# First matrix product of four 512-token tiles by Strassen's seven block products, weight sums streamed from memory

## The chip, the cores and the metric

The kernel runs on one core of one Trainium2 chip. The metric is device time in microseconds (us), the median of three runs. The engines are called PE (TensorE), DVE (VectorE), ACT (ScalarE), POOL (GpSimd) and SP (SyncE, which issues the DMAs).

## What is computed

The reference first computes decay attention with 4 batches, 8 heads, 768 positions and head size 64, in blocks with a carried state, then a feed-forward layer on all 3072 tokens:

```python
def _moe_ref(x, w_in, w_out):          # x 3072 x 512, w_in 512 x 2048, w_out 2048 x 512
    h = np.maximum(x @ w_in, 0.0)
    return (h * h @ w_out).astype(np.float32)
```

The change concerns the product `x @ w_in` alone.

## The kernel before

A **chunk** is 128 tokens of one batch; there are 24. The constant `SIZES` groups them into eight tiles, of 2, 3, 3, 3, 3, 3, 3 and 4 chunks. Tiles are numbered from 0. For each tile, attention fills `xh` and `xl`, a high and a low part of x whose sum is x to float32 accuracy; the weights stay in SBUF in the same two parts (`wih`, `wil`, `woh`, `wol`), each in 16 blocks of 128 hidden units. For each hidden block f, `ffn` issues:

- **first product**, `mm1` (L566): three part products (xh wih, xl wih, xh wil) of four contraction blocks each, 12 matmuls. The weight block stands still in the array and the tile's tokens stream through it: 384 columns in a tile of three chunks, 512 in one of four. The sum lies in one PSUM bank.
- **relu and square**: ACT relu out of the bank (L582), ACT square into the high part (L587), DVE square (L588), DVE low part (L589).
- **second product**, `mm2` (L572, L573, L575): for each chunk three matmuls of 512 columns into that chunk's output bank. From tile 2 on the second products of two f are issued together.

An attention chunk of the later tiles is a **turn** (`turn_over`): the scores and state updates of one chunk (L401, L408) and the values of the chunk before it (L417, L424), 128 matmuls on 64x64 pieces of the array, with DVE and ACT work behind them (L508 to L535) and a weighted copy of the next chunk's values on DVE (L439) whose data SP loads (`pn`, L442). Finished output rows are copied out of PSUM (L633) and stored (L634).

The order on each engine is made ahead of the run by a small list scheduler, `Plan.order`, from keys and estimated durations; each engine then runs its own list strictly in order. PSUM has eight banks for all of this, `in` has four load buffers.

```python
for wt, xt in ((wih[f], xh), (wih[f], xl), (wil[f], xh)):
    for cc in range(NCC):
        nc.tensor.matmul(at(h)[:, 0:n], wt[:, cc, :], xt[:, cc, 0:n], start=k == 0, stop=k == 3 * NCC - 1)
```

Of the kernel before, what the change touches and what calls it, by code (L numbers as in the profile page):

```python
# [745 lines left out]
```

## Time and profile before

| what | value |
|---|---|
| median of 3 runs | 603.98 us (603.98 to 604.13) |
| profiled execution | 603.77 us, its span 602.1 us |
| PE busy | 595.3 us (99%) |
| PE weight loads busy | 528.2 us (88%) |
| DVE busy | 312.3 us (52%) |
| ACT busy | 221.6 us (37%) |
| DMA | 49.08 MB, mean 82 GB/s |

The span runs from the first to the last instruction of the profiled execution; the 1.67 us between it and that execution's time lie outside. A matmul's recorded duration is longer than its share of the engine, since matmuls overlap: what one costs is the distance from its start to the next one's.

### The profile page before, as it was taken

How to read it: one execution, taken by the hardware profiler on the slowest of the kernel's cores; microseconds unless marked ns; L12 is line 12 of the kernel's file. 1: busy time of each engine (PE TensorE's matmuls, PEld its weight loads, DVE VectorE, ACT ScalarE, POOL GpSimd, SP SyncE). 2: the span in 40 equal slices, each digit the busy share in tenths (PEclk: the TensorE clock that was granted, in tenths of full speed). 3: DMA queues.
4: the chain of work that ended last, by engine and by line, in shares of the span. 5: the costliest groups of instructions: out<-in, count | busy, mean ns of one | idle time of the engine just before them, and what ended most of it. 6: DMA issues, size and time to landing. Idle time of an engine off the chain costs nothing.

```text
span 602.1 us, 12963 instructions
## 1 busy us (share of the span) xinstructions
PE 595.3 (99%) x5646; PEld 528.2 (88%) x5646; DVE 312.3 (52%) x665; ACT 221.6 (37%) x470; POOL 4.2 (1%) x12
## 2 busy tenths in 40 slices
PE   8999999999999999999999999999999999999997
PEld 6899889889899898998998998988988988888885
DVE  6999999756534435524454343443555432322132
ACT  5877877534223232322322323322322322222221
POOL 2000000000000000000000000000000000000000
PEclk9999999999999999999999999999999999999999
DMA  8845655443210202201122021210231000100001
GB/s 293 307 139 175 204 182 186 165 159 124 89 39 33 71 36 89 72 0 72 52 72 71 1 72 53 72 71 1 71 124 36 3 0 1 53 1 1 0 1 70
DMA packets 15897, 49.08 MB, mean 82 GB/s; under 512 B 1888, under 2 KB 2144, under 8 KB 15840
## 3 DMA queue, kind: packets, MB, share of 16 engines
q1 hardware_dynamic: 15840, 48.25, 23.2%
q8 instruction: 44, 0.72, 0.5%
q14 instruction: 13, 0.11, 0.1%
HBM read 41.95 MB, written 6.29 MB: 80 GB/s over the span
## 4 chain that ended last, share of the span: by engine, by line
PE 91%; DVE 4%; DMA 2%; ACT 2%; issue 1%; ACTq 0%; DVEq 0%; SPq 0%
PE bank L566 42%; PE bank L572 14%; PE bank L575 14%; PE bank L573 14%; PE bank L401 2%; PE bank L417 2%; PE bank L424 2%; PE bank L408 1%; DMA in<-pn 1%; PE bank L264 1%; DVE m L329 1%; DMA in<-w 1%; DVE m L331 1%; ACT half L437 1%; DVE gls L589 1%
## 5 line engine op out<-in xcount | busy, mean ns | idle before, releaser
L572 PE MATMUL bank<-woh,ghs 128*128 128x512 f32 x352 | 139.3, 396 | 0.7 <-ACT ghs L585 0.7
L573 PE MATMUL bank<-wol,ghs 128*128 128x512 f32 x352 | 137.5, 391 | 0.0
L588 DVE TENSOR_TENSOR g<-g 128x384 f32<-128x384 f32 x80 | 44.7, 558 | 151.8 <-ACT ghs L587 151.8
L566 PE MATMUL bank<-xh,wih 128*128 128x384 f32 (+2 forms) x512 | 111.1, 339 | 0.0
L582 ACT ACTIVATE g<-bank 128x384 f32<-128x384 f32 (+1 forms) x112 | 53.3, 476 | 155.3 <-PE bank L566 155.3
L566 PE MATMUL bank<-xh,wil 128*128 128x384 f32 (+2 forms) x512 | 109.6, 336 | 0.0
L566 PE MATMUL bank<-xl,wih 128*128 128x384 f32 (+2 forms) x512 | 109.5, 336 | 0.0
L566 PEld LDWEIGHTS bank<-xh,wih 128*128 128x128 f32 x512 | 89.2, 188 | 6.3
L575 PE MATMUL bank<-woh,gls 128*128 128x512 f32 x352 | 92.8, 390 | 0.0
L566 PEld LDWEIGHTS bank<-xh,wil 128*128 128x128 f32 x512 | 88.6, 188 | 2.7
L566 PEld LDWEIGHTS bank<-xl,wih 128*128 128x128 f32 x512 | 88.5, 188 | 2.7
L572 PEld LDWEIGHTS bank<-woh,ghs 128*128 128x128 f32 x352 | 66.1, 188 | 14.4 <-ACT ghs L585 1.3
L575 PEld LDWEIGHTS bank<-woh,gls 128*128 128x128 f32 x352 | 65.9, 188 | 13.9
L573 PEld LDWEIGHTS bank<-wol,ghs 128*128 128x128 f32 x352 | 66.1, 188 | 12.1
L589 DVE TENSOR_TENSOR gls<-g,ghs 128x384 fp32r<-128x384 f32 (+1 forms) x112 | 60.2, 538 | 18.2 <-ACT ghs L585 9.8
L587 ACT ACTIVATE ghs<-g 128x384 fp32r<-128x384 f32 x80 | 42.0, 525 | 43.8 <-PE bank L573 42.1
L588 DVE TENSOR_TENSOR half<-half 128x512 f32<-128x512 f32 x16 | 11.1, 692 | 55.4 <-ACT ghs L587 28.1
L582 ACT ACTIVATE half<-bank 128x512 f32<-128x512 f32 x16 | 9.6, 601 | 58.3 <-PE bank L566 55.3
L530 ACT COPY half<-bank 128x256 f32<-128x256 f32 x40 | 12.9, 376 | 46.1 <-PE bank L424 46.1
L324 ACT ACTIVATE m<-in 128x512 f32<-128x512 f32 x32 | 21.7, 678 | 10.5 <-DMA in<-w 5.3
L531 DVE TENSOR_TENSOR half<-bank,half 128x256 f32<-128x256 f32 x40 | 15.1, 419 | 13.3 <-ACT half L530 13.2
L329 DVE SCALAR_TENSOR_TENSOR m<-in,m 128x512 uint32<-128x512 uint32 x32 | 21.7, 685 | 0.1
(75 smaller groups left out, 468.3 us busy)
## 6 DMA issues: line engine op xcount, KB each, us to landing
in<-pn SPq DMA_DIRECT2D x44, 512.0 KB, 4.5
in<-w SPq DMA_DIRECT2D x32, 512.0 KB, 3.8
out<-obs SPq DMA_DIRECT2D x22, 256.0 KB, 2.1
half<-pn SPq DMA_DIRECT2D x8, 256.0 KB, 5.0
out<-m SPq DMA_DIRECT2D x1, 256.0 KB, 2.0
out<-m SPq DMA_DIRECT2D x2, 128.0 KB, 1.7
g<-lamx SPq DMA_DIRECT2D x1, 8.0 KB, 1.6
```

What stands on the lines that cost most here:

```text
L324: o = add("ACT", 0.58, lambda: nc.scalar.activation(at(m), words(1).bitcast(F32), AF.Abs), [o], [st, m])
L329: o = add("DVE", 0.6, lambda: nc.vector.scalar_tensor_tensor(out=bits(), in0=words(1), scalar=0xC0000000, in1=bits(), op0=ALU.bitwise_and, ...
L530: oc = [add("ACT", 0.27, 1, lambda r=r: nc.scalar.copy(x4(xr)[:, 2 * r:2 * r + 2], at(ys[r])[:, 0:2 * C].rearrange("p (v i) -> p v i", v=2 ...
L531: oa = [add("DVE", 0.36, 1, lambda v=v: nc.vector.tensor_tensor(out=by_v(x4(xr), v), in0=y_(ys, v), in1=by_v(x4(xr), v), op=ALU.add), oc, ...
L566: nc.tensor.matmul(at(h)[:, 0:n], wt[:, cc, :], xt[:, cc, 0:n], start=k == 0, stop=k == 3 * NCC - 1)
L572: nc.tensor.matmul(at(os_[j]), gh_()[:, sl], woh[f], start=f == 0, stop=False)
L573: nc.tensor.matmul(at(os_[j]), gh_()[:, sl], wol[f], start=False, stop=False)
L575: nc.tensor.matmul(at(os_[j]), gl_()[:, sl], woh[f], start=False, stop=f == NF - 1)
L582: orr = plan.op("ACT", ta, key - ahead, lambda: nc.scalar.activation(g_(), at(h)[:, 0:n], AF.Relu), [o1], [h, turn_, g])
L587: ogh = plan.op("ACT", ta, key, lambda: nc.scalar.activation(gh_(), g_(), AF.Square), [orr], [g] + gs[:1], before)
L588: og = plan.op("DVE", tv, key, lambda: nc.vector.tensor_tensor(out=g_(), in0=g_(), in1=g_(), op=ALU.mult), [orr, ogh], [g])
L589: ogl = plan.op("DVE", tv, key - ahead, lambda: nc.vector.tensor_tensor(out=gl_(), in0=g_(), in1=gh_(), op=ALU.subtract), [og, ogh], [g] + ...
```

## The change

The 24 chunks are regrouped into seven tiles, of 2, 3, 3, 4, 4, 4 and 4 chunks. Tiles 0 to 2 are worked as before. In tiles 3 to 6 the first product goes by Strassen's algorithm in its Winograd form, on 2x2 blocks: 256 tokens x 256 contraction elements x 128 hidden units. Two hidden blocks make a **pair** p, of which there are eight. In place of eight block products there are seven, each of six matmuls of 256 columns (three part products, two contraction blocks):

- `sums`, during tile 2, eight times: POOL rebuilds w_in of two hidden blocks from its parts (two adds), DVE forms four differences, ACT and DVE split them into two parts, and SP stores the plain blocks and the sums in a DRAM tile `wd`, 14 blocks of 256 columns (1.835 MB) for each pair.
- `combine`, once for a tile: attention leaves x unsplit (`raw`); DVE forms four sums and ACT and DVE split seven operands (L681, L684).
- `seven`, for each tile and pair: SP streams `wd[p]` into one of three buffers laid over the old w_in; PE computes the seven products in four groups g1 to g4 (12, 12, 6 and 12 matmuls, L719) into two banks X and Y. Between them ACT copies X (`o_t`) and DVE adds (`o_u`, `o_v`, `o_c22`, `c12`), since g3 and g4 add onto quarters that must have been read before. Then relu, square and split, and the second product in pieces of 12, 6 and 6 matmuls (L767).

The x buffers, the product's parts and the streams are laid over buffers of the first tiles.

```diff
-SIZES = (2, 3, 3, 3, 3, 3, 3, 4)
+SIZES = (2, 3, 3, 4, 4, 4, 4)
...
+PLAIN = 3
+Q = 2 * C
...
+    "vds": 2, "xr": 1, "raw": 1, "tst": 2, "st": 3, "gp": 2, "ms": 2, "big": 1, "sum": 1, "u": 1}
...
+COMBOS = ("A12", "S4", "A22", "A11", "S2", "S1", "S3")
...
+BLOCKS = {"B11": (0, 2), "B21": (1, 3), "B22": (4, 5), "T1": (6, 10), "T4": (7, 11), "T3": (8, 12), "T2": (9, 13)}
+WP = 14 * Q
...
+    wd = [dram.tile([P, WP], U32, name=f"wd{p}") for p in range(NF // 2)]
...
+        late = raw is not None or not alone
+        t, tv, vd, s1, xr = Buf("in"), Buf("in"), Buf("vds" if late else "half"), [Buf("s1") for _ in range(R)], raw or Buf("xr" if late else "half")
...
+            if raw is not None:
+                return [xo]
...
+    def sums(p, key):
...
+        oa = [plan.op("POOL", 1.1, key, lambda f=f, m=m: nc.gpsimd.tensor_tensor(out=at(m), in0=whole(f)[0], in1=whole(f)[1], op=ALU.add),
+                      list(ws[f][0]), [m]) for f, m in ((f0, ma), (f1, mb))]
...
+        o1 = minus(b11, b12, b11, oa, [ma, mb])
+        o3 = minus(b12, b22, b12, [o1], [mb])
+        o2 = minus(b22, b22, b11, [o3], [ma, mb])
+        o4 = minus(b21, b21, b22, [o2], [ma, mb])
+        oh = [plan.op("ACT", 0.53, key, lambda k=k, m=m: nc.scalar.copy(at(ts)[:, 2 * k * Q:2 * (k + 1) * Q], at(m)), [o], [m, ts]) for k, m, o in ((0, ma, o4), (1, mb, o2))]
+        ol = [plan.op("DVE", 0.6, key, lambda k=k, m=m: nc.vector.tensor_tensor(
+            out=at(ts)[:, (4 + 2 * k) * Q:(6 + 2 * k) * Q], in0=at(m), in1=at(ts)[:, 2 * k * Q:2 * (k + 1) * Q], op=ALU.subtract), [oh[k]], [m, ts]) for k, m in ((0, ma), (1, mb))]
+        os_ = [plan.op("SP", 1.45, key, lambda: nc.sync.dma_start(out=wd[p][:, 0:4 * Q], in_=words(win[:, f0 * 2 * DM:(f0 + 1) * 2 * DM])), list(ws[f1][0]), after=[steps[0, min(NF - 1, 2 * p + 4)]]),
+               plan.op("SP", 0.8, key, lambda: nc.sync.dma_start(
+                   out=wd[p][:, 4 * Q:6 * Q].rearrange("p (k i) -> p k i", k=2),
+                   in_=words(win[:, f1 * 2 * DM:(f1 + 1) * 2 * DM]).rearrange("p (k i) -> p k i", k=2)[:, :, Q:2 * Q]), list(ws[f1][0]), after=[steps[0, min(NF - 1, 2 * p + 4)]]),
+               plan.op("SP", 2.9, key, lambda: nc.sync.dma_start(out=wd[p][:, 6 * Q:], in_=words(at(ts))), oh + ol, [ts])]
...
+    def combine(ti, ready, raw, xc, before, key):
...
+        o1 = tt(s1_, A["A21"], A["A22"], ALU.add, ready, [raw, tmp])
+        o3 = tt(A["A21"], A["A11"], A["A21"], ALU.subtract, [o1], [raw])
+        d["A11"] = split("A11", A["A11"], ready, [raw])
+        o2 = tt(A["A11"], s1_, A["A11"], ALU.subtract, [o1, o3] + d["A11"], [raw, tmp])
+        d["S2"] = split("S2", A["A11"], [o2], [raw])
+        d["S1"] = split("S1", s1_, [o1], [tmp])
+        d["S3"] = split("S3", A["A21"], [o3], [raw])
+        d["A12"] = split("A12", A["A12"], ready, [raw])
+        o4 = tt(A["A12"], A["A12"], A["A11"], ALU.subtract, [o2] + d["A12"], [raw])
+        d["S4"] = split("S4", A["A12"], [o4], [raw])
+        d["A22"] = split("A22", A["A22"], ready, [raw])
...
+    def seven(ti, p, xc, d, os_, key, behind, carry):
+
+        st, X, Y, u, big, gp = Buf("st"), Buf("bank"), Buf("bank"), Buf("u"), Buf("big"), Buf("gp")
+        o_st = plan.op("SP", 5.2, key - 2.5 * 2 * FAST, lambda: nc.sync.dma_start(out=words(at(st)), in_=wd[p]), stored[p], [st], behind + [last_mm.get("stream")])
+        last_mm["stream"] = o_st
...
+                for a, b in ((0, 0), (0, 1), (1, 0)):
+                    for cc in range(2):
+                        nc.tensor.matmul(at(to)[:, i * Q:(i + 1) * Q], wt[a][:, cc, :], xt[b][:, cc, :], start=first and k == 0, stop=stop and k == 5, skip_group_check=True)
...
+        g1 = group([(X, 0, "A11", "B11", True, True), (X, 1, "S2", "T2", False, True)], key, [], [last_mm.get("seven")])
+        o_t = act(0.27, 0, lambda: nc.scalar.copy(quarter(u, 0), quarter(X, 0)), [g1], [X, u])
+        o_u = dve(0.33, 0, lambda: nc.vector.tensor_tensor(out=quarter(u, 1), in0=quarter(u, 0), in1=quarter(X, 1), op=ALU.add), [o_t], [X, u])
+        g2 = group([(Y, 0, "S1", "T1", True, True), (Y, 1, "S3", "T3", False, True)], key + 0.1, [], [g1])
+        o_v = dve(0.33, 0.1, lambda: nc.vector.tensor_tensor(out=quarter(u, 2), in0=quarter(u, 1), in1=quarter(Y, 0), op=ALU.add), [o_u, g2], [Y, u])
+        o_c22 = dve(0.33, 0.1, lambda: nc.vector.tensor_tensor(out=quarter(big, 3), in0=quarter(u, 2), in1=quarter(Y, 1), op=ALU.add), [o_v], [Y, u, big])
+        g3 = group([(X, 0, "A12", "B21", False, True)], key + 0.6, [o_t, o_u], [g2])
+        g4 = group([(Y, 0, "S4", "B22", False, True), (Y, 1, "A22", "T4", False, True)], key + 0.7, [o_v, o_c22], [g3])
+        last_mm["seven"] = g4
+        steps[ti, p] = g1, g4
...
+        r22 = act(0.27, 0.6, lambda: nc.scalar.activation(quarter(big, 3), quarter(big, 3), AF.Relu), [o_c22], [big])
+        r11 = act(0.27, 0.6, lambda: nc.scalar.activation(quarter(big, 2), quarter(X, 0), AF.Relu), [g3], [X, big])
+        c12 = dve(0.6, 0.7, lambda: nc.vector.tensor_tensor(
+            out=quarter(big, 0, 2).rearrange("p (n i) -> p n i", n=2), in0=quarter(u, 1).unsqueeze(1).broadcast_to([P, 2, Q]),
+            in1=quarter(Y, 0, 2).rearrange("p (n i) -> p n i", n=2), op=ALU.add), [g4], [Y, u, big])
+        sq = act(0.53, 0.8, lambda: nc.scalar.activation(quarter(big, 2, 2), quarter(big, 2, 2), AF.Square), [r11, r22], [big])
+        h1 = act(0.53, 0.8, lambda: nc.scalar.copy(quarter(gp, 2, 2), quarter(big, 2, 2)), [sq], [big, gp])
+        l1 = dve(0.6, 0.8, lambda: nc.vector.tensor_tensor(out=quarter(gp, 6, 2), in0=quarter(big, 2, 2), in1=quarter(gp, 2, 2), op=ALU.subtract), [h1], [big, gp])
+        s0 = dve(0.6, 0.8, lambda: nc.vector.scalar_tensor_tensor(out=quarter(big, 0, 2), in0=quarter(big, 0, 2), scalar=0.0, in1=quarter(big, 0, 2), op0=ALU.max, op1=ALU.mult), [c12], [big])
+        h0 = act(0.53, 0.9, lambda: nc.scalar.copy(quarter(gp, 0, 2), quarter(big, 0, 2)), [s0], [big, gp])
+        l0 = dve(0.6, 0.9, lambda: nc.vector.tensor_tensor(out=quarter(gp, 4, 2), in0=quarter(big, 0, 2), in1=quarter(gp, 0, 2), op=ALU.subtract), [h0], [big, gp])
...
+        ab = [[(j, k) for j in range(4) for k in range(2) if (place(j, k)[0] >= 2) == x] for x in (True, False)]
+        if p < NF // 2 - 1 or ti < len(TILES) - 1:
+            for x, (what, deps, dk) in enumerate(((ab[0], [h1, l1], 0.2), (ab[1][:2], [h0, l0], 0.8), (ab[1][2:], [h0, l0], 0.9))):
+                last_mm["second"] = o = plan.op(
+                    "PE", 0.685 * len(what), key + 2 * FAST + dk, lambda what=what, x=x: second(what, p == 0 and x == 0), deps, [gp] + os_, [last_mm.get("second")])
...
+            u = unit(b, c, xs[ti], j * C, key, 0.0 if ti - 1 - (j == 0) >= PLAIN else 4.0, steps[0, BEHIND] if ti == 2 else None, raw=raws[ti])
...
+                early = [o for p in range(NF // 2) for o in sums(p, begin[2] + 15 + p * 6.0)]
+            d = combine(ti, ready, raws[ti], xc, [], begin[ti] - 8.0)
...
+                seven(ti, p, xc, d, os_, begin[ti] + 2 * p * FAST, behind, None)
...
+    for ti in range(PLAIN, len(TILES) - 1):
+        for p in range(0, NF // 2, 2):
+            o, k = turns[k], k + 1
+            o.after.append(steps[ti, p][1])
+            steps[ti, p + 1][0].after.append(o)
```

The order changes in three places that the prediction speaks of. On PE, a step of the four-chunk tile 7 before stands thus (12 matmuls of the first product, then 12 of the second, of which the first three and the first L575 are shown):

```order
L566 MATMUL bank_65<-xh_101,wih_111 128x512 x4
L566 MATMUL bank_65<-xl_102,wih_111 128x512 x4
L566 MATMUL bank_65<-xh_101,wil_127 128x512 x4
L572 MATMUL bank_64<-woh_142,ghs 128x512 [waits Activation_49]
L573 MATMUL bank_64<-wol_158,ghs 128x512
L575 MATMUL bank_64<-woh_142,gls 128x512 [waits DVE_49]
```

and now, a pair of tile 3 that follows a turn (bank_75 is X, bank_74 is Y):

```order
L719 MATMUL bank_75<-xall,win 128x256 [waits DMAHW4_49,DVE_49]
L719 MATMUL bank_75<-xall,win 128x256 x11
L719 MATMUL bank_74<-xall,win 128x256 [waits DVE_49,Activation_49]
L719 MATMUL bank_74<-xall,win 128x256 x11
L719 MATMUL bank_75<-xall,win 128x256 [waits DVE_49]
L719 MATMUL bank_75<-xall,win 128x256 x5
L767 MATMUL bank_78<-woh_110,win 128x512
L767 MATMUL bank_78<-wol_126,win 128x512
L719 MATMUL bank_74<-xall,win 128x256 [waits DVE_49]
L719 MATMUL bank_74<-xall,win 128x256 x11
```

The groups g1, g2 and g3 stand directly behind one another, and g3 waits for DVE's read of X; six matmuls of the pair before stand between g3 and g4 (two are shown). In the other pairs twelve such matmuls stand between g2 and g3.

On ACT, the steps of the last three-chunk tiles before are relu and square in turn:

```order
L582 ACTIVATE g_71<-bank_68 128x384 [waits PE_49]
L534 CAST xh_99<-half_94 128x4x128 [waits DVE_49,Activation_49]
L587 ACTIVATE ghs<-g_71 128x384 [waits Activation_49]
L582 ACTIVATE g_73<-bank_64 128x384 [waits PE_49]
L587 ACTIVATE ghs<-g_73 128x384 [waits Activation_49]
```

and now, at the end of tile 3, from the copy of X of pair 7 on (L684 splits an operand of the next tile; L750 and L749 are relu, L754 square, L755 the high part that the second product waits for, L758 the other high part):

```order
L739 COPY gs<-bank_75 128x256 [waits DVE_49,PE_49]
L684 CAST xall<-halfs 128x512
L684 CAST xall<-ms 128x512 [waits DVE_49,PE_49]
L750 ACTIVATE ms<-bank_75 128x256 [waits DVE_49,PE_49]
L684 CAST xall<-halfs 128x512
L749 ACTIVATE ms<-ms 128x256 [waits DVE_49]
L684 CAST xall<-halfs 128x512 [waits Activation_49]
L754 ACTIVATE ms<-ms 128x512 [waits Activation_49]
L684 CAST xall<-halfs 128x512
L755 CAST win<-ms 128x512 [waits Activation_49]
L684 CAST xall<-halfs 128x512 [waits PE_49]
L758 CAST win<-ms 128x512 [waits DVE_49]
```

Between relu out of PSUM and the high part now stand three splits of the next tile's x.

On SP, the loads for two turns before stand alone:

```order
L442 DMA in_81<-pn 128x1024 [waits DMAHW5_49,DMAHW2_49,PE_49]
L442 DMA in_82<-pn 128x1024 [waits PE_49]
L442 DMA in_81<-pn 128x1024 [waits DMAHW2_49,DMAHW4_49,DVE_49,PE_49]
L442 DMA in_83<-pn 128x1024 [waits PE_49]
L442 DMA in_81<-pn 128x1024 [waits DMAHW4_49,DMAHW6_49,DVE_49,PE_49]
```

and now two streams stand ahead of each turn's pair of loads:

```order
L709 DMA win<-wd_63 128x3584 [waits DMAHW1_49,PE_49]
L709 DMA win<-wd_64 128x3584 [waits DMAHW4_49,PE_49]
L458 DMA in_89<-pn 128x1024 [waits DMAHW6_49,DVE_49,PE_49]
L458 DMA in_91<-pn 128x1024 [waits DMAHW3_49,PE_49]
L709 DMA win<-wd_65 128x3584 [waits DMAHW5_49,PE_49]
L709 DMA win<-wd_66 128x3584 [waits DMAHW0_49,PE_49]
```

A load that follows a stream in the queue is issued after it, on the same DMA engines.

## Rows read from the trace of the kernel before

**Rows 1.** The page, parts 1 and 2: busy time, and PE's granted clock in 40 slices.
```profile
PE 595.3 (99%) x5646; PEld 528.2 (88%) x5646; DVE 312.3 (52%) x665; ACT 221.6 (37%) x470; POOL 4.2 (1%) x12
...
PEclk9999999999999999999999999999999999999999
```

**Rows 2.** The page, part 4: the chain that ended last, by engine.
```profile
PE 91%; DVE 4%; DMA 2%; ACT 2%; issue 1%; ACTq 0%; DVEq 0%; SPq 0%
```

**Rows 3.** Busy time of each engine by stretch: us, busy (count), clock, DMA share, GB/s.
```profile
150.00:250.00 100.00, 100.00 (x1009) 90.45 (x1011) 44.58 (x94) 28.55 (x59) 0.00 (x0) 1.00 0.16 54
...
350.00:500.00 150.00, 150.00 (x1544) 135.91 (x1537) 68.79 (x148) 43.17 (x91) 0.00 (x0) 1.00 0.15 51
500.00:586.00 86.00, 86.00 (x378) 70.54 (x377) 23.76 (x36) 20.96 (x35) 0.00 (x0) 1.00 0.03 10
```

**Rows 4.** The chain in order of time: start us, us, what.
```profile
195.28 4.16 PE bank L566 x24
...
202.17 1.36 PE bank L575 x6
203.53 0.62 PE bank L401 x32
...
205.56 0.43 PE bank L572
```

**Rows 5.** The same view, tile 7.
```profile
512.43 2.76 PE bank L566 x12
515.19 0.23 PE bank L572
...
517.04 0.92 PE bank L575 x4
517.96 2.76 PE bank L566 x12
```

**Rows 6.** Timeline of PE in tile 0: start us, us, instructions.
```profile
83.47 0.64 PE L566 MATMUL bank<-xh,wih 128*128 128x256 f32 x4
83.94 0.63 PE L566 MATMUL bank<-xl,wih 128*128 128x256 f32 x4
84.42 0.63 PE L566 MATMUL bank<-xh,wil 128*128 128x256 f32 x4
84.89 0.40 PE L572 MATMUL bank<-woh,ghs 128*128 128x512 f32 x1
```

**Rows 7.** The same view, tile 0 with the DMA busy.
```profile
28.12 0.63 PE L566 MATMUL bank<-xl,wih 128*128 128x256 f32 x4
28.48 0.54 PEld L566 LDWEIGHTS bank<-xh,wil 128*128 128x128 f32 x4
28.60 0.63 PE L566 MATMUL bank<-xh,wil 128*128 128x256 f32 x4
```

**Rows 8.** Groups by line and shape: count, busy us, mean ns, idle before.
```profile
L566 PEld LDWEIGHTS bank<-xh,wih 128*128 128x128 f32 x512 | 89.2, 188 | 6.3
...
L531 DVE TENSOR_TENSOR half<-bank,half 128x256 f32<-128x256 f32 x40 | 15.1, 419 | 13.3 <-ACT half L530 13.2
...
L530 ACT COPY half<-bank 128x256 f32<-128x256 f32 x40 | 12.9, 376 | 46.1 <-PE bank L424 46.1
...
L588 DVE TENSOR_TENSOR half<-half 128x512 f32<-128x512 f32 x16 | 11.1, 692 | 55.4 <-ACT ghs L587 28.1 <-ACT wih L587 27.3
...
L587 ACT ACTIVATE ghs<-half 128x512 fp32r<-128x512 f32 x8 | 5.0, 631 | 2.4 <-PE bank L573 2.2
...
L260 POOL TENSOR_TENSOR tables<-g 128x8 f32<-128x8 f32 x1 | 1.6, 1642 | 0.1
```

**Rows 9.** Timeline in tile 3: first product, then the ACT relu that waits for it.
```profile
315.45 0.86 PE L566 MATMUL bank<-xh,wih 128*128 128x384 f32 x4
...
315.65 0.49 ACT L582 ACTIVATE g<-bank 128x384 f32<-128x384 f32 x1 [1.03 <-PE bank L566]
```

**Rows 10.** Timeline behind a turn: ACT and DVE.
```profile
204.71 0.80 SPq L442 DMA_DIRECT2D in<-pn  x2
205.61 0.65 ACT L530 COPY half<-bank 128x256 f32<-128x256 f32 x2 [2.82 <-PE bank L424]
206.29 0.76 DVE L531 TENSOR_TENSOR half<-bank,half 128x256 f32<-128x256 f32 x2 [0.86 <-ACT half L530]
...
209.53 0.68 DVE L439 TENSOR_TENSOR half<-in,tables 128x512 f32<-128x512 f32 x1
```

**Rows 11.** Stretches of the start with the DMA at its fullest, columns as in rows 3.
```profile
9.00:15.00 6.00, 5.26 (x136) 3.99 (x134) 5.92 (x16) 4.89 (x18) 0.00 (x0) 1.00 0.99 340
15.00:20.00 5.00, 4.98 (x143) 4.51 (x144) 5.00 (x15) 4.51 (x17) 0.00 (x0) 1.00 1.03 409
```

**Rows 12.** The page, part 6: DMA issues, KB each, us from issue to landing.
```profile
in<-pn SPq DMA_DIRECT2D x44, 512.0 KB, 4.5
```

More of the change, by code (lines that the diff above doesn't have):

```diff
@@ L58 @@
 class Plan:
-    LAT = {"PE": 0.25, "ACT": 0.15, "DVE": 0.12, "POOL": 0.12, "SP": 2.0}
+    LAT = {"PE": 0.25, "ACT": 0.15, "DVE": 0.12, "POOL": 0.12, "SP": 2.0, "NONE": 0.01}
     def __init__(self):
@@ L545, in unit, with rows_out @@
         return dict(key=key, front=Part(dur_f, front, dep_f, buf_f), begin=begin_, values=Part(dur_v, both, [o_vd] + o_old, buf_v), back=back)
-    last_mm, steps, tail = {}, {}, []
+    last_mm, steps, copied = {}, {}, {}
+    def rows_out(ti, j, o_done, os_, key):
+        b, c = TILES[ti][j]
+        nt, last = len(TILES[ti]), ti == len(TILES) - 1
+        ob = Buf("vds" if last and j >= nt - 2 else "ob")
+        parts = [slice(0, DM // 2), slice(DM // 2, DM)] if last and j == nt - 1 else [slice(0, DM)]
+        for k, sl in enumerate(parts):
+            eng, fn = (("DVE", nc.vector.tensor_copy), ("ACT", nc.scalar.copy))[(j + k) % 2]
+            o = plan.op(eng, 0.6 / len(parts), key, lambda fn=fn, sl=sl: fn(at(ob)[:, sl], at(os_[j])[:, sl]), [o_done], [os_[j], ob])
+            plan.op("SP", 0.75 / len(parts), key, lambda sl=sl: nc.sync.dma_start(
+                out=out[b * S + c * C:b * S + (c + 1) * C, sl], in_=at(ob)[:, sl]), [o], [ob])
     def ffn(ti, f, x, ready, wo, os_, key, held):
@@ new lines, in combine, with tt, split @@
+    def combine(ti, ready, raw, xc, before, key):
+        A = {n: (lambda i=i: at(raw)[:, 2 * i * Q:2 * (i + 1) * Q]) for i, n in enumerate(("A11", "A12", "A21", "A22"))}
+        tmp = Buf("sum")
+        s1_ = lambda: at(tmp)
+        def tt(out_, a, b, op, deps, bufs, after=()):
+            return plan.op("DVE", 0.6, key, lambda: nc.vector.tensor_tensor(out=out_(), in0=a(), in1=b(), op=op), deps, bufs, after)
+        def split(n, a, deps, bufs):
+            oh = plan.op("ACT", 0.53, key, lambda: nc.scalar.copy(at(xc[n])[0], a()), deps, bufs + [xc[n]], before)
+            ol = tt(lambda: at(xc[n])[1], a, lambda: at(xc[n])[0], ALU.subtract, [oh], bufs + [xc[n]])
+            return [oh, ol]
+        d = {}
+        o1 = tt(s1_, A["A21"], A["A22"], ALU.add, ready, [raw, tmp])
[9 more added lines that the diff above has]
+        d["A22"] = split("A22", A["A22"], ready, [raw])
+        return d
@@ L705, with gate @@
             ffn(ti, f, x, ready, ws[f], os_, begin[ti] + (f - f % 2 if two else f) * per[ti], held)
+    def gate(late, early):
+        kinds = lambda o: {b.kind for b in o.bufs}
+        first = [o for o in plan.ops if kinds(o) & set(early)]
+        then = [o for o in plan.ops if kinds(o) & set(late)]
+        g = plan.op("NONE", 0.0, 0, lambda: None, first)
+        for o in then:
+            o.after.append(g)
+    k = SIZES[2] + SIZES[3] + 1
+    for ti in range(PLAIN, len(TILES) - 1):
[3 more added lines that the diff above has]
+            steps[ti, p + 1][0].after.append(o)
+    assert k == len(turns)
+    gate(["vds"], ["half"])
+    gate(["raw"], ["half", "xr"])
+    gate(["tst"], ["x1"])
+    gate(["ms"], ["m"])
+    gate(["big", "sum"], ["m", "ms"])
+    gate(["u"], ["g"])
+    gate(["xA12", "xS4", "xA22"], ["x0"])
+    gate(["xA11", "xS2", "xS1", "xS3"], ["x1", "tst"])
+    o = plan.op("NONE", 0.0, 0, lambda: None, [steps[2, f] for f in range(NF)] + early)
+    for q in plan.ops:
+        if any(b.kind == "gp" for b in q.bufs):
+            q.after.append(o)
     for i, key in EARLY:
```

180 lines of the change are left out of this document (114 added, 66 removed), and 2 rows, old and new, of the table EARLY.

## The prediction

> **What bounds the kernel now.** I read the page first: PE is busy 99% of the span at the upper of its two clock levels (2.4 GHz) in all 40 slices, DVE 52%, ACT 37% [rows 1]. The chain that ended last is 91% PE [rows 2]. Then the stretches: from 150 us on PE has no idle time at all, DVE is busy 45 to 46 us in 100 and falls to 28% in tile 7, and the DMA share is at most 0.16 [rows 3]. So behind 150 us whatever is taken from PE's list comes off the time, as long as nothing new makes PE wait. Last I read what a matmul costs, as the distance between starts: 24 of 384 columns take 4.16 us (173.3 ns each) and six of 512 take 1.36 us (227 ns) [rows 4]. In the four-chunk tile, 12 of 512 columns take 2.76 us (230 ns), and 12 of the second product take 517.96 - 515.19 = 2.77 us (230.8 ns) [rows 5]. 256 columns occur in tile 0 alone: 12 in 84.89 - 83.47 = 1.42 us, 118.3 ns each [rows 6]; with the DMA busy four take 0.48 us, 120 ns [rows 7]. All of these include a new weight block for each matmul.
>
> **The change, part by part.**
>
> *First product.* Before, the last 16 chunks take 768 matmuls of 384 columns (tiles 3 to 6) and 192 of 512 (tile 7): 768 x 0.1733 + 192 x 0.230 = 133.1 + 44.2 = 177.3 us. Now there are 4 tiles x 8 pairs x 42 = 1344 of 256 columns: 159.0 us at 118.3 ns, 161.3 at 120. Eight products become seven, but the short matmul costs 0.462 ns a column against 0.451, which takes back part of the eighth. Saved: **18.3 us**, at worst 16.0. I take 118.3, the quiet rows, since the streams fill less than half of the DMA's time (below).
>
> A rule speaks against this. Each weight load is recorded at 188 ns, whatever streams behind it [rows 8]. The Trainium skill, "Perfetto Trace Analysis", section "Identifying the Most-Contended Engine", judges TensorE by the summed time of its weight loads. By that sum a pair has 66 loads x 0.188 = 12.4 us against 10.4 us of matmul distance, and 32 pairs would be some 63 us longer, not shorter. Rows 6 and 7 disagree: 12 loads went by in 1.42 us and the next group of four began 0.48 us after the last, so loads overlap each other. By the trace the term stays.
>
> *Second product.* 768 matmuls of 512 columns before and after. They went at 227 ns in three-chunk tiles and 231 in tile 7; 576 of them now move to the four-chunk form: 0 to 576 x 0.0035 = 2.0 us. I take **+0.8**, nearer to the first, as their order is mixed.
>
> *The pair's own chain.* In the tightest pairs only g2 (1.42 us) lies between g1 and g3, which adds onto what ACT copied and DVE added. ACT starts 0.20 us behind the last matmul's turn [rows 9], copies in 0.376 us, DVE starts 0.03 us later (205.61 + 0.65 to 206.29) [rows 10] and adds in 0.419 [rows 8]; with 0.05 us to PE, an estimate like DVE's start, that is 1.08 us. It fits with 0.34 us to spare: **0**. The rest of a pair's DVE work, 3 x 0.419 + 4 x 0.692 = 4.0 us, and ACT's, 3 x 0.376 + 3 x 0.631 = 3.0 us, lie beside 10.4 us of PE.
>
> *Tile ends, three times.* The seven operands of the next tile are split between the last pair's own steps. From the last turn's end PE has 18 x 0.2275 (second product) + 30 x 0.1183 (g1 to g3) + 6 x 0.2275 + 12 x 0.1183 (g4) + 6 x 0.2275 = 11.8 us until it wants pair 7's high and low parts. g3 ends at 7.65 us; ACT then has relu, split, relu, split, square, split and high part in line, 2 x 0.376 + 5 x 0.631 = 3.9 us, and DVE 0.69 us: 7.65 + 0.20 + 3.9 + 0.03 + 0.69 + 0.05 = 12.5. Late by 0.7 us, three times: **+2.1**. Bounds: nothing, if ACT's starts overlap, and 1.7 us each if DVE stands one more step behind.
>
> *Streams and turns, twelve times.* A pair's weights are 1.835 MB: 4.5 us at the 409 GB/s of the start, 5.4 us at 340 [rows 11], under a period of 10.4 us or more, with three buffers; PE doesn't wait for them. But the values of the next turn are loaded behind two streams on SP, and DVE weights them (L439) ahead of `o_u` of the next pair, so if that load is late, g3 is. The load is issued 0.85 us before the turn's end (204.71 against 205.56) [rows 4, 10] and takes 4.5 us [rows 12], of which 512 KB at full rate are 1.3 to 1.5; a stream issued when g4 frees its buffer, 3.4 us before the turn's end, lands at 4.1 to 5.0 us behind it, the load at 5.4 to 6.5. Weighted 0.68 us later and `o_u` 0.42 after that, against g3 at 18 x 0.2275 + 24 x 0.1183 = 6.9 us: late by 0 to 0.7 us. I take 0.15, near the faster end, since the copies with long rows resemble the fullest stretch: **+1.8**, bounds 0 and 8.4.
>
> *Sums in tile 2.* Eight times 4 x 0.419 + 2 x 0.692 = 3.1 us, 24.5 us more on DVE within 74 us of PE time, where DVE now does some 33; with the first `combine` (7 us) it is 87% full, and in order behind 16 POOL adds. No row has such an add: the nearest are DVE's of that size (0.69 us) and POOL's only tensor operation (1.64 us for 8 columns) [rows 8]. At 0.69 nothing waits; at 2.3 (both summed) each set takes 8.3 us from POOL's start to the last split, 66 us in all, and could push tile 3 back by up to 5 us. Tile 2's second products stand 4 us behind DVE's part, so I take **+0.5**. The stores of plain blocks (6.3 MB) begin while the weights load in tiles 0 and 1, where DVE is the fuller engine: 0, up to 2.
>
> *The end.* Behind the last g4, the parts need 0.20 + 0.69 + 0.60 + 0.69 + 0.63 + 0.69 + 0.1 = 3.6 us; 12 matmuls cover 2.7: **+0.9**. Turns, copies and stores are as many as before.
>
> Sum on the profiled execution: 603.77 - 18.3 + 0.8 + 2.1 + 1.8 + 0.5 + 0.9 = 591.6 us. The median of the runs is 0.2 us above it, so I predict **591.8 us**. All terms at their gain ends give 586.
>
> **The rivals.**
>
> *All hidden* (0.18): the late steps above overlap, and only the 18.3 and a little at the end count: 585 to 589 us. For it: PE's 0.34 us of slack and DVE's 36% of free time. Against it: engines run in order, and the ACT line at a tile's end is full by count.
>
> *Queue lateness* (0.12): turns lose 0.7 us each and tile ends 1.7, 603.98 - 18.3 + 0.8 + 8.4 + 5.1 + 1.5 = 601.5 us; half of it, 595 to 597, is as likely. For it: each turn's load now stands behind a stream. Against it: 10 us of cover in most pairs.
>
> *The chain takes the bound* (0.04, slower): g3 or g4 waits in every pair, since ACT's copy of X stands behind the low half's copy of the pair before (L758), which waits for DVE. Above 13.4 / 32 = 0.42 us a pair the gain is gone; at 1 us the time is 592 + 32 = 624 us. Against it: six second-product steps lie between, and 1.08 us against 1.42.
>
> *Weight loads bind* (0.01, slower): loads would not overlap in pairs as they do in tile 0: 592 + 63 = 655 us. It is the rule named above; rows 6 contradict it.
>
> *No change* (0.02): the terms of the lateness add up to the gain, 603 to 605 us.
>
> **How the numbers follow.** The forecast itself, 589 to 595 us, has 0.63. The measurement tells 0.2% (1.2 us) from no change. Faster: 0.63 + 0.18 + 0.12 = 0.93; same 0.02; slower 0.05. The range of 8 in 10 takes the forecast, most of the hidden case and half of the lateness: **586.5 to 598.5 us**.
>
> **What would show it.** The L719 matmuls at 118 to 120 ns; PE idle in tiles 3 to 6 of some 4 us, before the first L767 of pair 7 with ACT or DVE as releaser and before g3 behind a turn, released by L740; DVE's weighting (L455) waiting for `pn`. The prediction is wrong if L719 stands at 130 ns or more, if PE idles over 10 us from tile 3 on, or if tile 2 ends later than it would now.

## The result, and the profile after

The changed kernel takes **597.18 us** (median of 4 runs, 594.59 to 598.11) against 603.98 us on the same chip: ratio 0.988, 95% interval 0.9849 to 0.9911. Run again on another chip, it took 595.63 us against 604.33 (0.9865, 0.9847 to 0.9883). So it is 7 to 9 us faster, where 12.2 had been forecast: inside the range of 586.5 to 598.5 us, outside the 589 to 595 us of the forecast itself. The profiled execution took 598.11 us, its span 596.4 us; it is the slowest of the four, so a loss read from its trace lies at the upper end.

The page, parts 1 and 4 [rows 1, 2]:

```profile
PE 581.8 (98%) x6030; PEld 517.2 (87%) x6030; DVE 385.8 (65%) x803; ACT 245.4 (41%) x532; POOL 29.1 (5%) x28
...
PE 64%; DVE 16%; DMA 10%; ACT 5%; issue 3%; POOL 1%; POOLq 0%; SPq 0%; ACTq 0%; DVEq 0%
```

The chain was 91% PE; now a third of it is other work, though PE is still busy 98% of the span. Where, the stretches tell (columns as in rows 3). First one of the kernel before that was not shown, then three of the changed one:

```profile
50.00:150.00 100.00, 99.83 (x958) 90.10 (x957) 84.35 (x184) 63.20 (x133) 0.00 (x0) 1.00 0.49 169
```

```profile
50.00:150.00 100.00, 94.84 (x920) 83.03 (x920) 82.05 (x174) 60.96 (x131) 4.56 (x3) 1.00 0.67 220
...
150.00:250.00 100.00, 98.69 (x1088) 88.57 (x1087) 82.89 (x167) 37.91 (x80) 20.35 (x14) 1.00 0.68 250
...
250.00:500.00 250.00, 249.06 (x2733) 222.82 (x2732) 138.48 (x288) 81.97 (x173) 0.00 (x0) 1.00 0.55 202
```

PE, which idled 0.17 us between 50 and 150 us, now idles 5.16 there, 1.31 between 150 and 250 (before: nothing [rows 3]), and 0.94 in the 250 us of Strassen's tiles. By idle time the tiles that were changed lose least; the tiles ahead of them, whose products were not touched, lose most. Idle time is only the least that a wait costs. A matmul's recorded duration is longer than its share of PE (L719: 280 ns in the mean on the page, at a distance of 118), so part of a wait lies under the record of the matmul ahead of it and shows as no idle time. The chain in order of time shows what stands there:

```profile
47.30 6.15 DMA in<-w
...
69.45 5.88 DMA in<-w
...
89.22 4.68 DMA in<-w
...
105.22 4.59 DMA in<-w
...
203.29 1.54 POOL ms L656
...
243.00 2.12 PE bank L719 x18
245.12 2.76 PE bank L767 x12
247.88 2.83 PE bank L719 x24
250.71 2.76 PE bank L767 x12
...
258.16 6.94 DMA in<-pn
265.13 0.69 DVE halfs L455
265.82 0.34 DVE gs L740
266.21 0.97 PE bank L719 x6
...
584.16 8.21 PE bank L767 x36
```

Three things are on it that were not forecast to cost much: loads of w in tiles 0 and 1, a POOL add of the sums in tile 2, and the load of a turn's values behind a stream. Between them lies what was forecast: 24 of Strassen's matmuls in 2.83 us, 117.9 ns each [rows 6 had 118.3], 12 of the second product in 2.76 us (230 ns), and 36 in 8.21 us at the end, 228 ns each with no gap.

The waits (engine, what it wanted, on whom: us in total, times, longest), of before and of the changed kernel:

```profile
ACT m L324 <- DMA in<-w: 5.3, 5, 2.8
```

```profile
PE bank L719 <- DVE gs L740: 0.9, 2, 0.5
...
ACT ms L343 <- DMA in<-w: 14.7, 9, 3.2
...
DVE halfs L455 <- DMA in<-pn: 23.2, 11, 4.1
...
DVE ms L654 <- POOL ms L656: 5.0, 3, 2.4
```

And the groups of the second product by line (page, part 5; the last figure is PE's idle time ahead of them):

```profile
L767 PE MATMUL bank<-woh,win 128*128 128x512 f32 x512 | 171.2, 393 | 0.0
...
L767 PE MATMUL bank<-wol,win 128*128 128x512 f32 x256 | 100.2, 391 | 0.0
```

The theories that follow: **S**, the stores of plain blocks, which run while the weights load, make those loads late; **P**, the sums cost in tile 2, through POOL; **T**, the turns' loads behind the streams cost in tiles 3 to 6. Two of the sixteen adds, at 118.78 and 125.33 us, already run in tile 1, so P reaches into the stretch of S.

### The profile page after: what moved, and what is told of

Same layout as the page of the kernel before. It is cut to its first block, busy times and chain, and to the rows that moved or that the text cites. A ratio compares the mean times of both kernels' runs of the same rounds, so it can differ in the third digit from the quotient of the medians.

```text
span 596.4 us, 14063 instructions
## 1 busy us (share of the span) xinstructions
PE 581.8 (98%) x6030; PEld 517.2 (87%) x6030; DVE 385.8 (65%) x803; ACT 245.4 (41%) x532; POOL 29.1 (5%) x28
## 4 chain that ended last, share of the span: by engine, by line
PE 64%; DVE 16%; DMA 10%; ACT 5%; issue 3%; POOL 1%; POOLq 0%; SPq 0%; ACTq 0%; DVEq 0%
PE bank L767 28%; PE bank L719 25%; DMA in<-pn 6%; DMA in<-w 5%; PE bank L595 3%; DVE gls L618 2%; DVE ms L348 2%; DVE ms L350 1%; PE bank L417 1%; PE bank L604 1%; DVE ms L654 1%; PE bank L601 1%; POOL ms L656 1%; PE bank L602 1%; DVE halfs L455 1%
## 5 line engine op out<-in xcount | busy, mean ns | idle before, releaser
L719 PEld LDWEIGHTS bank<-xall,win 128*128 128x128 f32 x1344 | 167.4, 188 | 6.9 <-DVE gs L740 1.8
L719 PE MATMUL bank<-xall,win 128*128 128x256 f32 x1344 | 170.4, 280 | 0.9 <-DVE gs L740 0.9
L767 PE MATMUL bank<-woh,win 128*128 128x512 f32 x512 | 171.2, 393 | 0.0
L767 PEld LDWEIGHTS bank<-woh,win 128*128 128x128 f32 x512 | 96.1, 188 | 19.3
L767 PE MATMUL bank<-wol,win 128*128 128x512 f32 x256 | 100.2, 391 | 0.0
L595 PE MATMUL bank<-xall,win 128*128 128x384 f32 (+1 forms) x576 | 95.2, 319 | 0.9 <-ACT gs L611 0.6
L595 PEld LDWEIGHTS bank<-xall,win 128*128 128x128 f32 x576 | 90.6, 188 | 3.8 <-ACT gs L611 0.8
L767 PEld LDWEIGHTS bank<-wol,win 128*128 128x128 f32 x256 | 48.1, 188 | 7.6
L601 PE MATMUL bank<-woh,ghs 128*128 128x512 f32 x128 | 51.2, 400 | 2.9 <-ACT ghs L614 1.4
L602 PE MATMUL bank<-wol,ghs 128*128 128x512 f32 x128 | 50.5, 394 | 1.1 <-DVE wol L353 1.1
L758 ACT CAST win<-ms 128x512 fp32r<-128x512 f32 x32 | 19.9, 621 | 52.5 <-DVE ms L757 52.5
L604 PE MATMUL bank<-woh,gls 128*128 128x512 f32 x128 | 36.0, 393 | 1.8 <-DVE gls L618 1.8
L750 ACT ACTIVATE ms<-bank 128x256 f32<-128x256 f32 x32 | 12.3, 384 | 54.6 <-PE bank L719 54.6
L749 ACT ACTIVATE ms<-ms 128x256 f32<-128x256 f32 x32 | 13.3, 416 | 42.2 <-DVE ms L743 42.2
L455 DVE TENSOR_TENSOR halfs<-in,tables 128x512 f32<-128x512 f32 x19 | 15.2, 802 | 23.2 <-DMA in<-pn 23.2
```

Of the source, the lines that this page charges most:

```text
L455: nc.vector.tensor_tensor(out=heads(at(vd)), in0=v_(), in1=wdec.unsqueeze(2).broadcast_to([P, H, D]), op=ALU.mult)
L601: nc.tensor.matmul(at(os_[j]), gh_()[:, sl], woh[f], start=f == 0, stop=False)
L602: nc.tensor.matmul(at(os_[j]), gh_()[:, sl], wol[f], start=False, stop=False)
L604: nc.tensor.matmul(at(os_[j]), gl_()[:, sl], woh[f], start=False, stop=f == NF - 1)
L719: nc.tensor.matmul(at(to)[:, i * Q:(i + 1) * Q], wt[a][:, cc, :], xt[b][:, cc, :], start=first and k == 0, stop=stop and k == 5, skip_grou ...
L767: nc.tensor.matmul(at(os_[j]), a, wt[2 * p + k], start=first and part == 0 and wt is woh, stop=p == NF // 2 - 1 and part == 1 and not firs ...
```

## The experiments

Ratios are to the kernel before, run on the same chip in between; 0.0017 is 1 us.

**The changed kernel again**, as the base for what follows.

> The changed kernel once more, on the same chip as the next three, so that they are compared with it: 596 to 598 us, with a spread of some 3 us between its runs.

595.63 us, 594.61 to 598.54; ratio 0.9865 (0.9847 to 0.9883).

### The stores

**Stores alone, in the kernel before.** The weights of the first product lie in one tile, as after the change, and 16 stores of it are added; nothing reads them:

```diff
+    for p in range(NF // 2):
+        f0, f1 = 2 * p, 2 * p + 1
+        plan.op("SP", 1.45, ..., out=wd[p][:, 0:1024], in_=win[...], ..., after=[steps[0, min(NF - 1, 2 * p + 4)]])
+        plan.op("SP", 0.8, ..., out=wd[p][:, 1024:1536]..., in_=win[...], ..., after=[steps[0, min(NF - 1, 2 * p + 4)]])
```

> The kernel before with one part of the change alone: the 16 stores of plain blocks at the places in the queue that they have in the changed kernel; nothing reads them. Theory S: 4 to 6 us slower than before, 608 to 610 us, lost ahead of 150 us. Theories P and T: within 0.5 us of 604.0 us.

608.94 us against 604.32: **4.6 us slower** (ratio 1.0075, 1.0063 to 1.0087). Its stretch, then DMA issues by line between 50 and 120 us (KB each, us to landing), before and with the stores:

```profile
50.00:150.00 100.00, 97.40 (x936) 86.13 (x935) 81.83 (x180) 60.96 (x130) 0.00 (x0) 1.00 0.69 230
```

```profile
in<-w SPq DMA_DIRECT2D x18, 512.0 KB, 3.7
```

```profile
in<-w SPq DMA_DIRECT2D x19, 512.0 KB, 4.7
```

A load of w takes 1.0 us longer, and ACT's wait for these loads grows from 5.3 to 10.3 us. The four load buffers go round in a ring (load, ACT, DVE, free again), so a longer load is a longer round. That the ring is the way by which the stores cost is argued: no run changes the number of buffers. The weights' lying in one tile is not the cause, for the last kernel below has them so and idles 0.35 us in this stretch. Theory S holds, at the size expected here.

**Stores behind the loads.**

```diff
-after=[steps[0, min(NF - 1, 2 * p + 4)]]
+after=[steps[1, min(NF - 1, 11 + p // 2)]]
```

> The 16 stores of plain weight blocks (6.3 MB) are moved from tiles 0 and 1, where they stand between the weight loads on SP, to behind the last weight load (after steps 11 to 15 of tile 1). Theory S (the stores hold up the weight loads and with them PE): PE's busy time in 50 to 150 us returns by 4 to 5 us, ACT's waiting of L343 for the loads of w falls from 14.7 us to about the 5.3 us of before, and the time to 592 to 593.5 us. Theory P (the sums in tile 2 are what costs) and theory T (the turns behind the streams): no change, 596.5 to 598 us. If the stores then hold up the loads of tile 2 or the stores of the sums, part of the gain comes back behind 150 us.

601.02 us (0.9941, 0.9926 to 0.9956): **slower than the changed kernel by some 4 us**, a miss. The first half of the expectation came true: a load of w lands in 3.5 us, ACT's wait for them falls to 7.4 us. But now the loads of tile 2's and 3's inputs stand among the stores. In the kernel before, four of them landed in 3.9 us each between 120 and 140 us; here (DMA issues of that stretch, then the chain):

```profile
wd<-win SPq DMA_DIRECT2D x7, 512.0 KB, 6.5
in<-pn SPq DMA_DIRECT2D x4, 512.0 KB, 7.2
```

```profile
171.86 11.19 DMA in<-pn
183.08 0.69 DVE halfs L455
```

One load stays 11.19 us on the chain. PE idles 4.51 us between 50 and 150 us and 4.57 between 150 and 250. Part of the loss is the clock: from 155 to 160 us it was granted at 0.71, behind 9.4 us (145 to 154.4) in which PE was busy 4.96. The warning at the end of the expectation came true and outweighed the gain.

**Stores on ACT's queue.** The same two operations with `nc.scalar.dma_start` on ACT instead of `nc.sync.dma_start` on SP.

> The 16 stores of plain weight blocks keep their place in time but go out on ACT's DMA queue instead of SP's. Theory SQ (they cost because the loads of w behind them stand in the same queue, first in, first out): 3 to 4.6 us faster than the changed kernel, 592.5 to 594 us, and ACT's waiting of L343 for loads of w falls from 12 to 15 us to 8 us or less. Theory SB (they cost because the DMA engines have no time to spare while the weights load): within 1 us of the changed kernel, the waiting unchanged.

598.47 us (0.9908, 0.9892 to 0.9924), not faster but some 2.6 us slower than the changed kernel's second run on the same chip, which neither theory had expected. Loads of w between 50 and 120 us, here and in that second run:

```profile
in<-w SPq DMA_DIRECT2D x18, 512.0 KB, 4.3
```

```profile
in<-w SPq DMA_DIRECT2D x19, 512.0 KB, 4.5
```

ACT waits 11.0 us for them, there 10.9. So the place in SP's queue is not what costs (theory SQ falls); the transfers share the DMA engines whichever engine issues them. The Trainium skill, "DMA: Bandwidth & Descriptors", section "Issuing engines are not separate DMA queues", says so, and this run agrees. The order on ACT was planned anew here, so the loss against the changed kernel isn't put down to anything.

**Fewer stores.** Only pair 0's plain blocks are stored, and every stream reads them:

```diff
-        os_ = [plan.op("SP", 1.45, ...), plan.op("SP", 0.8, ...), plan.op("SP", 2.9, ...)]
+        plain = [plan.op("SP", 1.45, ...), plan.op("SP", 0.8, ...)] if p == 0 else []
+        os_ = plain + [plan.op("SP", 2.9, ...)]
...
-        o_st = plan.op("SP", 5.2, ..., in_=wd[p])
+        o_st0 = plan.op("SP", 2.2, ..., in_=wd[0][:, 0:6 * Q])
+        o_st = plan.op("SP", 3.0, ..., in_=wd[p][:, 6 * Q:])
```

> Leaves out 14 of the 16 stores of plain blocks (those of pairs 1 to 7; every stream takes its plain half from pair 0's copy, as two transfers with the bytes of one). The rest of the queue ahead of the streams keeps its order. Theory S: 7/8 of the 4.6 us that the stores cost in the kernel before, 4 us off 595.6 to 597.2 us: 591.5 to 593.5 us, ratio to before 0.979 to 0.982. If the stores cost little in the changed kernel: 595 us or more.

591.03 us, ratio 0.9785 (0.9771 to 0.9799): 0.0080 below the changed kernel's 0.9865, **4.8 us**, somewhat more than expected. The stretches show the gain between 50 and 150 us, and that the loss of tile 2 (1.15 us) stays:

```profile
50.00:150.00 100.00, 97.96 (x942) 86.33 (x940) 86.45 (x183) 62.91 (x135) 5.84 (x4) 1.00 0.54 173
...
150.00:250.00 100.00, 98.85 (x1092) 89.23 (x1093) 80.32 (x161) 37.83 (x80) 18.50 (x12) 1.00 0.67 249
```

But not all of the gain is the stores'. The streams come as two transfers here, and behind 250 us PE idles no more either. In the two profiles tile 3 begins (first L719) at 226.20 us in the changed kernel and at 222.53 here: 3.7 us, which the stores can have cost. From there to the end of the span it is 370.2 us against 368.1: another 2.1, which belong to theory T (below). Why the turns lose nothing here was not tested.

### The sums

**No arithmetic for the sums** (ACT copies for the adds, no subtractions):

```diff
-oa = [plan.op("POOL", 1.1, key, lambda f=f, m=m: nc.gpsimd.tensor_tensor(out=at(m), in0=whole(f)[0], in1=whole(f)[1], op=ALU.add), ...
+oa = [plan.op("ACT", 0.55, key, lambda f=f, m=m: nc.scalar.copy(at(m), whole(f)[0]), ...
...
-        o1 = minus(b11, b12, b11, oa, [ma, mb])
-        o3 = minus(b12, b22, b12, [o1], [mb])
-        o2 = minus(b22, b22, b11, [o3], [ma, mb])
-        o4 = minus(b21, b21, b22, [o2], [ma, mb])
+        o4, o2 = oa
```

> Leaves out the arithmetic of the weight sums: the 16 POOL adds become ACT copies of the high parts and the 32 subtractions on DVE of 256 columns fall away; the splits, the stores and the streams stay as they are. Theory P: 2.5 to 5 us faster than the changed kernel, 592 to 594.7 us, gained between 150 and 225 us. Theory S: under 1.5 us faster, 595.7 to 597.5 us. Theory T: no change.

593.22 us (0.9807, 0.9788 to 0.9826): theory P's value. PE is busy 50.00 of 50 us from 150 to 200 and from 200 to 250 us.

**What in them costs.** The timeline of the changed kernel in tile 2, POOL and then DVE (start us, us, instructions, idle time ahead):

```profile
193.86 1.30 POOL L656 TENSOR_TENSOR ms<-win 128x512 f32<-128x512 f32 x1 [3.33 <-DVE xall L664]
...
203.29 1.54 POOL L656 TENSOR_TENSOR ms<-win 128x512 f32<-128x512 f32 x1 [3.16 <-DVE xall L664]
...
194.03 0.75 DVE L550 TENSOR_TENSOR halfs<-bank,halfs 128x256 f32<-128x256 f32 x2
...
203.13 0.55 DVE L617 TENSOR_TENSOR gs<-gs 128x384 f32<-128x384 f32 x1
203.59 1.78 DVE L664 TENSOR_TENSOR xall<-ms,xall 128x512 fp32r<-128x512 f32 x1
```

The L664 that begins 0.30 us after POOL's add ends 0.54 us after the add's end, as if it had only begun as the add ended; alone it takes 0.69 us. The L617 that was under way when the add began keeps its 0.55 us, and there it is the add that takes 1.54 us and not 1.30. The two L550 that fall wholly beside an add take 0.75 us for both, as ever: they read a PSUM bank and one SBUF tile, L664 and L617 read SBUF alone. Groups by line and shape on DVE between 118 and 206 us, first the changed kernel, then the one with the adds on DVE (below):

```profile
L664 DVE TENSOR_TENSOR xall<-ms,xall 128x512 fp32r<-128x512 f32 x14 | 11.5, 837 | 2.3 <-ACT xall L663 2.3
L617 DVE TENSOR_TENSOR gs<-gs 128x384 f32<-128x384 f32 x11 | 9.6, 871 | 0.2 <-ACT ghs L616 0.2
```

```profile
L656 DVE TENSOR_TENSOR ms<-win 128x512 f32<-128x512 f32 x15 | 10.0, 686 | 0.1
L664 DVE TENSOR_TENSOR xall<-ms,xall 128x512 fp32r<-128x512 f32 x14 | 9.4, 688 | 1.6 <-ACT xall L663 1.4
...
L617 DVE TENSOR_TENSOR gs<-gs 128x384 f32<-128x384 f32 x11 | 6.1, 555 | 0.5 <-ACT ghs L616 0.4
```

L617 takes 871 ns in the mean beside POOL and 555 without it, L664 837 and 688. This is what the Trainium skill states in "SBUF — State Buffer", section "🔬 SBUF: two separate sides": DVE and GpSimd share a pair of SBUF ports, a GpSimd operation that reads SBUF and a DVE operation with two SBUF inputs exclude each other, and whichever starts first keeps the ports to its end. The rows agree that the two exclude each other and, for all adds but one, that the first to start goes on to its end. The exception is the add at 118.78 us: it took 2.28 us, and a DVE operation (L353) that began 0.10 us behind it kept its 0.69. The ports themselves no row shows.

**Adds on DVE.**

```diff
-plan.op("POOL", 1.1, key, lambda f=f, m=m: nc.gpsimd.tensor_tensor(...
+plan.op("DVE", 0.6, key, lambda f=f, m=m: nc.vector.tensor_tensor(...
```

> The 16 adds of the sums run on DVE instead of POOL. In the profile of the changed kernel DVE operations that begin beside a POOL add take 1.4 to 1.8 us where they take 0.55 to 0.69 alone, some 9.6 us in total. Theory L (POOL's adds block DVE): DVE takes on 16 x 0.69 = 11.0 us and gets 9.6 us back, and each sum is some 0.8 us shorter, so the time is the same or up to 1.5 us shorter, 595.5 to 597.5 us. Theory W (DVE is only short of time for its own work): 1 to 3 us slower, 598 to 600 us.

592.15 us (0.9802, 0.979 to 0.9815), **3.5 us faster** than the changed kernel on the same chip: more than theory L had allowed. The page shows why it costs DVE nothing:

```profile
PE 580.3 (98%) x6030; PEld 517.5 (87%) x6030; DVE 385.5 (65%) x819; ACT 246.2 (42%) x532; POOL 4.2 (1%) x12
```

DVE does 16 instructions more, some 11.0 us at 686 ns, in 385.5 us against 385.8. So about as much of its busy time had been standing still. DVE's 5.0 us of waiting for the adds (the last of the waits above) are gone too. The run takes both away at once, so how the 3.5 us divide between operations held up beside an add and DVE waiting in order for its end is not shown. PE is busy all of 150 to 250 us.

**Copies for POOL's adds, subtractions kept**: the first piece of the diff of the kernel without arithmetic alone.

> Leaves out the 16 POOL adds alone (ACT copies of the high parts stand in their place); the 32 subtractions on DVE stay. Theory L: almost all that leaving out the sums' whole arithmetic gave, 3 to 4 us faster than the changed kernel, 593 to 594.5 us. Theory W: 0 to 1.5 us faster, 595.5 to 597.5 us.

593.13 us (0.9815, 0.9802 to 0.9827), no different from the run without any arithmetic. DVE's 32 subtractions cost nothing that shows; POOL's adds are the price of the sums. PE's list is the changed kernel's here, matmul for matmul, so the two traces can be laid side by side. Tile 3 begins thus, first in the changed kernel, then here:

```profile
226.20 0.40 PE L719 MATMUL bank<-xall,win 128*128 128x256 f32 x2
```

```profile
220.98 0.40 PE L719 MATMUL bank<-xall,win 128*128 128x256 f32 x2
```

Of these 5.2 us, 1.5 come in one step at 127.81 us, in tile 1 behind the add at 125.33, and 2.2 in tile 2. The other 1.5 have nothing to do with the adds: that far the two executions lie apart at 98 us, ahead of the first add.

### The turns

**Weighting later.** Each turn's `o_vd` (L455) of tiles 4 to 6 waits for the first group of the pair ahead of its turn:

```diff
+            if vds[k]:
+                vds[k].after.append(steps[ti, p][0])
             o, k = turns[k], k + 1
```

> In tiles 3 to 5 the weighting of the next turn's values (L455) is put behind the first group of the pair that precedes that turn, so DVE no longer stands at it while the load comes in behind a stream. Theory T: DVE's 23.2 us of waiting at L455 fall below 5 us, PE's idle time behind the turns goes, and the time falls by 1.5 to 2.5 us to 595 us. Theories S and P: DVE's waiting goes as well, but the time stays at 596.5 to 598 us.

594.71 us (0.9842, 0.983 to 0.9855), theory T's value. DVE's wait at L455 falls from 23.2 to 0.9 us and PE waits for nothing behind 225 us. The interval overlaps the changed kernel's, so the medians leave the size uncertain: 2.3 us against its first runs, 1.4 against its second. The traces settle it, since from tile 3 on PE's list is the same, matmul for matmul. Here tile 3 begins with

```profile
224.64 0.40 PE L719 MATMUL bank<-xall,win 128*128 128x256 f32 x2
```

and the span is 592.8 us. From this matmul to the end of the span it is 368.2 us; in the changed kernel's two profiles it is 370.2 (596.4 - 226.20) and 370.6. So **the turns cost 2.0 to 2.5 us**. Between the first of these and this run the difference grows in five steps, each at an L719 behind a turn (the first is 266.21 in the chain above). PE's idle time in 250 to 500 us, 0.94 us, shows less than half of it.

### Together

**Both mends** (adds on DVE, weighting later).

> The changed kernel with the adds of the sums on DVE and the weighting of the next turn's values behind the first group of the pair ahead of that turn. The two losses lie in different stretches (tile 2, and the turns of tiles 3 to 5); if so, the gains add: 3.5 us and 2 us off 596 to 597, 590 to 591.5 us, ratio to before 0.976 to 0.979. If they were the same loss, seen twice: no better than the adds on DVE alone, 592 to 593 us.

592.00 us (0.979, 0.9768 to 0.9812): the fastest complete kernel together with the next, 12 us faster than before. By its time it can't be told from the adds on DVE alone (0.9802), and it misses the 590 to 591.5 us expected. The traces show the turns' gain all the same: from tile 3's first L719 to the end of the span it is 370.0 us with the adds on DVE alone and 368.1 here. Its profile has no idle PE left from 150 to 500 us:

```profile
50.00:150.00 100.00, 97.53 (x936) 85.53 (x936) 85.29 (x183) 62.36 (x133) 0.00 (x0) 1.00 0.68 226
...
150.00:250.00 100.00, 100.00 (x1102) 90.94 (x1102) 81.89 (x178) 38.64 (x80) 0.00 (x0) 1.00 0.69 251
250.00:500.00 250.00, 250.00 (x2739) 224.18 (x2738) 143.19 (x294) 84.61 (x177) 0.00 (x0) 1.00 0.56 206
```

**And two pairs' stores in tile 2.**

```diff
-after=[steps[0, min(NF - 1, 2 * p + 4)]]
+after=[steps[0, 2 * p + 4] if p < 6 else steps[2, 2 * p - 2]]
```

> The same, and the plain blocks of the last two pairs are stored in tile 2 (behind its steps 10 and 12) instead of beside the last weight loads; 1.5 of the 6.3 MB leave the stretch of the weight loads. By the price of all 16 stores (4.6 us): up to 1.2 us faster than the kernel with both mends. If tile 2, where the sums' stores and the first streams go, has no time on the DMA to spare either: the same or up to 1 us slower.

591.15 us, ratio 0.9792 (0.9777 to 0.9806): the same within the intervals. Inconclusive.

**Both mends and fewer stores.** Both diffs from above.

> The same with both mends (adds of the sums on DVE, weighting later). If the shortfall is the stores, the POOL adds and the turns, and these add up, the kernel stands where the forecast without late work had it: 603.98 - 18.3 + 0.8 to 1.7 + 0.9 = 587.4 to 588.3 us, and with an eighth of the stores left some 588 us (586.5 to 589.5), ratio 0.971 to 0.976. If something else is missing: 590 us or more.

**586.77 us** (0.9711, 0.9697 to 0.9724), where the sum without late work had stood. The stretch that had lost most is nearly whole again:

```profile
50.00:150.00 100.00, 99.65 (x955) 89.50 (x954) 88.73 (x193) 63.75 (x135) 0.00 (x0) 1.00 0.54 182
```

Against both mends with all stores the ratio is 0.0079 lower, 4.8 us; in the traces tile 3 begins at 217.15 us against 222.28, and from there on the two take the same 368.1 us. So it is the stores' price once more, the third way, and with no loss at the turns on either side.

## Why the prediction was right in its direction, and too high in its gain

- **First product, -18.3:** held. 117.9 ns a matmul with the streams running, and with POOL's adds, the turns' lateness and seven eighths of the stores taken away 586.77 us. Weight loads overlap as rows 6 had it; the rival in which they bind is refuted.
- **Second product, +0.8:** 230 ns within the pairs, 228 at the end, so between 0.6 and 1.7 us.
- **The pair's chain, 0:** held. PE's only waits for L740 are two, 0.9 us, and both stand behind a turn (265.82 in the chain is one). The rival that it binds falls. (In it the gain was gone above 12.2 / 32 = 0.38 us a pair, not 13.4 / 32; nothing hangs on it.)
- **Tile ends, +2.1, and the end, +0.9:** too high. PE does not wait before a single L767 in the whole profile (the groups above), and at the end 36 run without a gap. So ACT's seven steps at a tile's end, which I laid end to end, come early enough, the gain end of the first bound; which of them overlap was not read.
- **Turns, +1.8:** held, with 2.0 to 2.5 us, and the mechanism was right to the line: load behind a stream, L455 late, `o_u`, g3. PE's idle time alone, 0.94 us, would have said half of it.
- **Sums, +0.5:** one of two steps that failed. I bounded POOL's add by its own length, and it lies within the bounds (1.30 us alone, 1.57 in the mean). What I left out is that DVE, which I had 87% full there, is held up beside it. Moving the adds gave 3.5 us back, some of it in tile 1, where I had no sums. No row that I had read has POOL at work beside DVE, and I did not weigh the Trainium skill's rule named above.
- **Stores, "0, up to 2":** the other step that failed, and the larger. I read DVE as the fuller engine while the weights load, which it was, and took transfers to be free where the DMA share is 0.5. The stores lengthened a load of w from 3.7 to 4.7 us, and cost 4.6 us; ACT's wait for these loads grew from 5.3 to 10.3 us. The round of four buffers, which I had left out, would explain it, though no run varied it.

With the measured sizes the sum is 603.8 - 18.3 + 1.2 + 0 + 2.1 + 3.5 + 4.6 = 596.9 us (second product, tile ends and the end, turns, sums, stores), against medians of 597.18 and 595.63.

The rival named "queue lateness, half" gave 595 to 597 us, the time that was found, for another reason: turns and tile ends lost 2.1 us together, not the 6.8 that half of its 8.4 and 5.1 make. The number alone would have confirmed a wrong story, and it was luck that a range wide enough for that rival also held the stores and the adds. Of the three signs that I had set for an error, the third came true: the first product of tile 2 ends at about 222 us, before at 214. The other two, in Strassen's own tiles, did not.

Left open: how the price of the adds divides, why the turns lose nothing where a stream comes as two transfers, and what the 0.35 us of idle PE that is left ahead of 150 us hangs on. A kernel that keeps all stores and loses nothing to them was not found; keeping some plain blocks resident was not tried.

## What to carry to other kernels

Cost what a change prepares (copies, sums, stores ahead of the stage that uses them) with the same care as the stage itself: here the stage gave nearly all of its 18 us, and the preparation took back 8. A transfer beside a stage that waits for loads in a short ring of buffers isn't free at half DMA load: price it by what it adds to each load, and expect it to cost wherever another such load stands. PE's idle time is the least that a wait costs: to price one, lay the traces of two kernels with the same PE list side by side and read where the distance between them grows. Work given to an idle POOL isn't free for a DVE that reads two SBUF operands, and with DVE at 65% the adds were cheaper there.
